# Where ScalarE's steps of a weight split stand in its queue, and how many blocks are split early

## The chip, the cores and the metric

One core of one Trainium2 chip. The metric is the device time of one execution in microseconds (us). TensorE does the matrix products, VectorE and ScalarE and GpSimd the elementwise work, SyncE (SP) issues nearly all DMAs. Each engine works through its own queue in program order and waits there for what its next instruction needs.

## What is computed

```python
def reference(q, k, v, moe_w_in, moe_w_out, moe2_...):
    # attention, 4 batches x 8 heads, 1152 keys, 576 queries (pairs of q rows averaged), head size 64
    q_pool = q.reshape(B, H, S // 2, 2, D).mean(axis=3)
    p = softmax(q_pool @ k.T / sqrt(D))
    x = (p @ v) as [2304 tokens, 512]
    # dense layers, 512 -> 2048 -> 512, weights are 64-bit floats
    h = x @ w_in
    x = (h * sigmoid(1.702 * h)) @ w_out
    # eight experts, 512 -> 1024 -> 512, for the tokens with x @ w_skip > 0
    y[token] = gate * (relu(x @ w1[e]) @ w2[e]) for e = argmax(x @ w_gate)
    return x + y
```

## The kernel before

Every matrix operand is kept as a high and a low float32 part, and a product is three matmuls (high x high, high x low, low x high). The weights of the dense layers come as 64-bit floats and must first be **split** into such pairs. DFF = 2048 is cut into 16 blocks fb; a block needs one piece of w_in (giving the tiles wih, wil) and one of w_out (woh, wol). These 32 pieces are the units u = 2 fb + k, 128 x 512 numbers each. `wload` brings a unit into one of three buffers wr by DMA on SP's queue, `wsplit` splits it: ten instructions, seven on VectorE (L463, L464, L451, L466, L467, L455, L459 in this order) and three on ScalarE: L461 (the absolute value into t2, first), L452 (the low part's scale, on what L451 has just made) and L458 (the high part's rounding, on what L467 made). `wsplit` issues L461 at once and returns seven functions; L452 is issued together with L451 by `low`, L458 together with the last VectorE instruction by `last`.

**Attention** runs over 16 pairs of heads, 14 units of work each. One loop over steps g of 14 x 16 and some more writes out the order by hand: in each step the score matmuls of a unit (L273, into one of two banks), the exponential (L274, ScalarE), the maxima of a later pair (L230, L233), the products with v of an earlier unit (L310), sums of E for the denominators (L288, L290, L69, GpSimd; on VectorE for the end of the last pair), and the denominators' matmuls (L326). `Agenda` holds further work to be issued at a given step: among it the early units of the split. With EARLY = 3 blocks, units 0 and 1 are spread over quiet steps of pairs 1 to 9, and units 2 to 5 over the last 19 steps and the two behind, five steps each. Each instruction stands in its engine's queue where the loop issues it.

**The dense layers** go over six chunks of tokens (768, 384, 256, 256, 256, 384). A step g is one piece of up to 384 tokens and one block fb; the first chunk has two pieces, so 32 steps. In a step `layer1` issues 12 matmuls (L577) into one of two banks h, then on ScalarE the sigmoid (L582), on VectorE g (L583), on ScalarE gh (L584), on VectorE gl (L586); `layer2` issues 9 matmuls (L601 to L603) for the piece of two steps before. In the first chunk the other units are split on the way: `fill(3)` ahead of gl and `fill(3)` or `fill(4)` behind it take the next functions of `blocks()`, which goes through the units in order and holds back the last two functions of a unit (L455; L458 and L459) into the next one. That is 13 functions per block fb, and 26 units have 182. From step 23 on the x tiles of the next chunk are loaded (SP), normalised by VectorE (L482) and split (L491, L495). Behind the first chunk the split's buffers are given up, and the gate weights (wg) are loaded into their place.

**The experts** come last and are not touched.

Of the kernel before, what the change touches and what calls it, by code (L numbers as in the profile page):

```python
# [9 lines left out]
F32 = mybir.dt.float32  # L10
# [9 lines left out]
P = 128  # L20
# [29 lines left out]
EARLY = 3  # L50
# [21 lines left out]
class Kernel:  # L72
# [54 lines left out]
    def attention(self, ctx):  # L127
# [217 lines left out]
        def weights(u, put):  # L345
            t = ld.tile([P, 3, 512], U32, name="t", tag="wt", bufs=1)
            for j, f in enumerate(self.wsplit(u, [t[:, 0], t[:, 1], t[:, 2]])):
                put(j, f)
# [8 lines left out]
        for u in range(2):  # L357
            g = NU * 1 + 3 + u * (NU * 3 + 6)
            ag.at(g, self.wload, u)
            ag.at(g + 6, weights, u, lambda j, f: quiet(AV_AT[3:], j, f))  # L360

        for u in range(2, 2 * EARLY):
            g, n = NU * (N - 1) - 5, u - 2
            ag.at(g - 13 + 4 * n if n < 3 else g + 7, self.wload, u)
            ag.at(g + 5 * n, weights, u, lambda j, f, g=g + 5 * n: ag.at(g + j * 5 // 7, f))
# [64 lines left out]
    def wsplit(self, u, tmp):  # L430

        nc, V = self.nc, self.nc.vector
# [4 lines left out]
        if a.dtype == F32:  # L439
# [4 lines left out]
            ]  # L444
# [4 lines left out]

        def low():  # L450
            V.scalar_tensor_tensor(t1, lo, 9, t1, op0=ALU.logical_shift_right, op1=ALU.bitwise_or)  # L451
            nc.scalar.activation(t1.bitcast(F32), t1, AF.Copy, scale=2.0 ** -43)  # L452

        def power():
            V.tensor_scalar(sg, t2, 0xFF800000, None, op0=ALU.bitwise_and)  # L455

        def last():
            nc.scalar.activation(hi_t, t2.bitcast(F32), AF.Copy)  # L458
            V.tensor_tensor(lo_t, t1.bitcast(F32), sg.bitcast(F32), op=ALU.mult)  # L459

        nc.scalar.activation(t2.bitcast(F32), hi.bitcast(F32), AF.Abs)  # L461
# [3 lines left out]
            low,  # L465
            lambda: V.tensor_scalar(t2, t2, 3, 0x3FFFF000, op0=ALU.logical_shift_left, op1=ALU.bitwise_and),  # L466
            lambda: V.scalar_tensor_tensor(t2, hi, 0xC0000000, t2, op0=ALU.bitwise_and, op1=ALU.bitwise_or),  # L467
            power,
            last,
# [27 lines left out]
    def ffn(self, ctx):  # L497
# [36 lines left out]
        def blocks():  # L534

            end = ()
            for u in range(2 * EARLY, 2 * NF):
                if u + 2 < 2 * NF:
                    self.wload(u + 2)
                a, b, c, d, e, *new = self.wsplit(u, [tp.tile([P, 512], U32, name=nm, tag=nm) for nm in ("t1", "t2", "sg")])  # L540
                yield from (a, *end[:1], b, c, d, *end[1:], e)
                end = new
            yield from end

        splits = blocks()

        def fill(k):
            for _ in range(k):
                f = fq.pop(0) if fq else next(splits, None)
                if f:  # L550
                    f()

# [503 lines left out]
```

## Time and profile before

| | us |
|---|---|
| median of 3 runs | 1069.68 |
| lowest and highest | 1064.24, 1069.93 |
| the profiled execution | 1067.2 |
| its span, first to last instruction | 1065.1 |
| TensorE busy | 1002.7 (94% of the span) |
| VectorE busy | 767.6 (72%) |
| ScalarE busy | 506.0 (48%) |
| GpSimd busy | 453.5 (43%) |
| mean granted TensorE clock | 0.980 of 2.4 GHz |

The profile is of one execution. Rows name the line, the engine (PE is TensorE, DVE VectorE, ACT ScalarE, POOL GpSimd), the operation, and output <- inputs by the program's names. Matmuls are pipelined, so their durations overlap, and a step is better read from the starts. A row of the timeline ends with the idle time ahead of it on its engine, and who ended it.

### The profile page before, as it was taken

To read this page: it belongs to the slowest core of one execution; us is meant where nothing else is said; L and a number is where in the kernel's file an instruction comes from. 1 tells how busy PE (TensorE), PEld (TensorE's weight loads), DVE (VectorE), ACT (ScalarE), POOL (GpSimd) and SP (SyncE) were. 2 spreads that over 40 slices of the span, in tenths; PEclk is the share of its full clock that TensorE was granted. 3 is DMA by queue.
4 is the path that set the end of the run, shared out by engine and by line. 5 is a ranking of instruction groups with operands and counts; after the bars stand their busy time and mean duration, and the time that the engine had idled before them with its cause. 6 is when DMAs were issued, how large, how long until landed. Compare 5 with 4: busy or idle time off the path is not lost. (4 is left out here: it accounts for less than half of the span.)

```text
span 1065.1 us, 19053 instructions
## 1 busy us (share of the span) xinstructions
PE 1002.7 (94%) x7002; PEld 789.9 (74%) x7002; DVE 767.6 (72%) x1643; ACT 506.0 (48%) x928; POOL 453.5 (43%) x306
## 2 busy tenths in 40 slices
PE   6999999999999998799998999999999997998894
PEld 4666767666776665587887898888889886866673
DVE  7667777778877778878988589787475564556834
ACT  2555555555555554555655322333333262456623
POOL 3698999999999988400000002011111004213112
PEclk9999999999999999999999999999999998998997
DMA  4232232223333321323333620212211234738401
GB/s 161 69 100 80 80 100 80 80 80 95 95 96 98 101 87 62 101 80 115 120 99 99 169 79 22 70 30 59 70 47 45 80 116 152 249 123 272 150 22 50
DMA packets 64323, 103.38 MB, mean 97 GB/s; under 512 B 18630, under 2 KB 34630, under 8 KB 64072
## 3 DMA queue, kind: packets, MB, share of 16 engines
q1 hardware_dynamic: 60148, 96.35, 28.5%
q0 software_dynamic: 3904, 5.15, 1.6%
q8 instruction: 69, 1.13, 0.5%
q14 instruction: 54, 0.44, 0.1%
q10 hardware_dynamic: 148, 0.30, 0.1%
HBM read 90.04 MB, written 17.35 MB: 101 GB/s over the span
## 5 line engine op out<-in xcount | busy, mean ns | idle before, releaser
L233 DVE TENSOR_REDUCE mx<-xs 128x1 f32<-128x384 f32 x432 | 212.9, 550 | 81.1 <-PE xs L230 76.7
L274 ACT ACTIVATE E<-ss 128x640 f32<-128x640 f32 (+1 forms) x224 | 174.1, 786 | 148.0 <-PE ss L273 125.3
L290 POOL TENSOR_TENSOR acc<-acc,E 128x640 f32<-128x640 f32 (+1 forms) x94 | 179.8, 1912 | 22.4 <-ACT E L274 18.6
L310 PE MATMUL av<-E,v 128*64 128x256 f32 (+1 forms) x1152 | 158.5, 415 | 0.0
L577 PE MATMUL h<-xh,wih 128*128 128x384 f32 (+1 forms) x448 | 142.7, 318 | 8.7 <-DVE g L583 6.3
L577 PE MATMUL h<-xl,wih 128*128 128x384 f32 (+1 forms) x448 | 140.7, 314 | 0.2
L577 PE MATMUL h<-xh,wil 128*128 128x384 f32 (+1 forms) x448 | 140.5, 314 | 0.0
L482 POOL TENSOR_TENSOR xa<-xraw 128x256 f32<-128x256 f32 (+1 forms) x16 | 14.2, 890 | 256.9 <-DMA xraw<-RD 251.4
L310 PEld LDWEIGHTS av<-E,v 128*64 128x64 f32 x1152 | 76.3, 137 | 56.8 <-issue 16.4
L603 PE MATMUL acc<-woh,gl 128*128 128x512 f32 x288 | 114.7, 398 | 0.0
L601 PE MATMUL acc<-woh,gh 128*128 128x512 f32 x288 | 114.5, 398 | 0.0
L602 PE MATMUL acc<-wol,gh 128*128 128x512 f32 x288 | 114.3, 397 | 0.0
L273 PE MATMUL ss<-qh,kh 64*128 64x320 f32 (+1 forms) x576 | 107.1, 339 | 7.7 <-ACT E L274 7.7
L230 PE MATMUL xs<-kh,qh 64*128 64x384 f32 x384 | 102.9, 390 | 7.8 <-ACT kh L210 7.2
L577 PEld LDWEIGHTS h<-xh,wih 128*128 128x128 f32 x448 | 84.9, 190 | 18.8 <-DVE g L583 11.1
L583 DVE TENSOR_TENSOR g<-h,g 128x384 f32<-128x384 f32 (+1 forms) x112 | 55.8, 498 | 59.4 <-ACT g L582 58.0
L273 PE MATMUL ss<-M,ONE 64*128 64x320 f32 (+1 forms) x576 | 95.1, 296 | 2.8 <-DMA M<-ml 2.6
L584 ACT ACTIVATE gh<-g 128x384 fp32r<-128x384 f32 (+1 forms) x112 | 53.8, 480 | 89.9 <-DVE g L583 89.9
L620 DVE CUSTOM_DVE_ANT_0 junk<-xs,wg 128x512 bf16<-128x512 f32 x135 | 94.8, 702 | 2.0
L582 ACT ACTIVATE g<-h 128x384 f32<-128x384 f32 (+1 forms) x112 | 49.2, 439 | 97.9 <-PE h L577 97.8
L273 PE MATMUL ss<-qh,kl 64*128 64x320 f32 (+1 forms) x576 | 92.6, 294 | 0.0
L273 PE MATMUL ss<-ql,kh 64*128 64x320 f32 (+1 forms) x576 | 92.6, 294 | 0.0
(195 smaller groups left out, 2070.2 us busy)
## 6 DMA issues: line engine op xcount, KB each, us to landing
stage<-w SPq DMA_DIRECT2D x40, 512.0 KB
qd<-qT SPq DMA_DIRECT2D x16, 576.0 KB
v<-v SPq DMA_DIRECT2D x16, 576.0 KB
kr<-kT SPq DMA_DIRECT2D x15, 576.0 KB
wr<-w_in SPq DMA_DIRECT2D x16, 512.0 KB
wr<-w_out SPq DMA_DIRECT2D x16, 512.0 KB
X<-xs SPq DMA_DIRECT2D x18, 256.0 KB
out<-xs SPq DMA_DIRECT2D x18, 256.0 KB
```

What stands on the lines that cost most here:

```text
L230: nc.tensor.matmul(ps[:, :384], q, k[:, part * 384:part * 384 + 384], start=True, stop=True)
L233: V.reduce_max(o, ps[:, :384], axis=AX.X)
L273: nc.tensor.matmul(ps[:, u, j * w:j * w + w], k[HALF[u]], q[HALF[u], qs], start=(n == 0), stop=(n == 3))
L274: nc.scalar.activation(place(p, i), ps[:, :, :len(kbs) * w], AF.Exp, scale=0.5 / D ** 0.5)
L290: G.tensor_tensor(d["a"], d["a"], place(p, i), op=ALU.add)
L310: nc.tensor.matmul(d["av"][HALF[u], :w], d["v"][:, u, kb], e[:, u, n * w:n * w + w], start=(kb == 0), stop=(kb == KB - 1))
L577: nc.tensor.matmul(h, a[:, d * P:d * P + P], x, start=(k == 0), stop=(k == 3 * ND - 1))
L583: V.tensor_tensor(g, h, g, op=ALU.mult)
L601: nc.tensor.matmul(acc[t], gh[:, ts], bh, start=(fb == 0), stop=False)
L602: nc.tensor.matmul(acc[t], gh[:, ts], bl, start=False, stop=False)
L603: nc.tensor.matmul(acc[t], gl[:, ts], bh, start=False, stop=(fb == NF - 1))
L620: V.tensor_tensor_reduce(out=junk, in0=R[grp[i]], in1=late["wg"][:, e], op0=ALU.mult, op1=ALU.add, scale=1.0, scalar=0.0, accum_out=R[grp] ...
```

## The change

EARLY becomes 2: units 2 and 3 are split in the last 20 steps of attention, eight steps apart, and the 28 units from fb = 2 on in the first chunk of the dense layers (196 functions of VectorE in place of 182). `wsplit` issues nothing itself; it returns VectorE's seven and ScalarE's three functions apart, and each caller places them. In attention, a unit's steps are: Abs at g - 1, VectorE's seven at g to g + 5 and g + 8, the low part's scale at g + 5 (three behind what makes its input), the high part's rounding at g + 7. The scratch tile gets two buffers. In the dense layers a list `after` collects ScalarE's functions when their inputs have been issued; `act()` issues all that are in it, in every step behind gh, and `need` does so earlier where VectorE's next function wants one that is still in the list. A unit is begun (`make`, with the load of the unit two ahead) in the middle of the one before it.

```diff
--- before.py
+++ after.py
@@ -47,7 +47,7 @@
 
 UNITS = [(0, (kb,)) for kb in range(KB)] + [(1, tuple(range(kb, min(kb + 2, KB)))) for kb in range(0, KB, 2)]
 NU = len(UNITS)
-EARLY = 3
+EARLY = 2
 AV_AT = (4, 7, 10, 13, 1)
 GROUPS = [range(0, 3), range(3, 6), range(6, 9), range(9, 12), range(12, 14)]
 
@@ -342,10 +342,11 @@
         start = {1: [(k_low, 0)], 2: [(q_low, 0)], 4: [(loads, 2)], 5: [(q_add, 1)], 7: [(q_high, 1)], 8: [(k_high, 1, 0)], 9: [(k_high, 1, 1)],
                  10: [(k_high, 1, 2)], 11: [(v_load, 0)], 13: [(q_add, 2)]}
 
-        def weights(u, put):
-            t = ld.tile([P, 3, 512], U32, name="t", tag="wt", bufs=1)
-            for j, f in enumerate(self.wsplit(u, [t[:, 0], t[:, 1], t[:, 2]])):
-                put(j, f)
+        def weights(u, steps):
+            t = ld.tile([P, 3, 512], U32, name="t", tag="wt", bufs=2)
+            v, a = self.wsplit(u, [t[:, 0], t[:, 1], t[:, 2]])
+            for g, f in zip(steps, (a[0], v[0], v[1], v[2], v[3], v[4], v[5], a[1], a[2], v[6])):
+                ag.at(g, f)
 
         def operands(j, pc):
             raw = ld.tile([P, 2, 384], F32, name="xraw", tag="xraw", bufs=1)
@@ -356,13 +357,14 @@
 
         for u in range(2):
             g = NU * 1 + 3 + u * (NU * 3 + 6)
+            calm = [x for x in range(g + 7, g + 5 * NU) if x % NU in AV_AT[3:]]
             ag.at(g, self.wload, u)
-            ag.at(g + 6, weights, u, lambda j, f: quiet(AV_AT[3:], j, f))
+            ag.at(g + 6, weights, u, [g + 6, *calm[:6], calm[4] + 1, calm[5] + 1, calm[6]])
 
         for u in range(2, 2 * EARLY):
-            g, n = NU * (N - 1) - 5, u - 2
-            ag.at(g - 13 + 4 * n if n < 3 else g + 7, self.wload, u)
-            ag.at(g + 5 * n, weights, u, lambda j, f, g=g + 5 * n: ag.at(g + j * 5 // 7, f))
+            g = NU * (N - 1) - 5 + 8 * (u - 2)
+            ag.at(g - 13, self.wload, u)
+            ag.at(g - 1, weights, u, [g - 1, g, g + 1, g + 2, g + 3, g + 4, g + 5, g + 5, g + 7, g + 8])
         for n in range(2):
             ag.at(NU * N - 8 + 5 * n, self.wload, 2 * EARLY + n)
         for b in range(8):
@@ -431,6 +433,7 @@
 
 
 
+
         nc, V = self.nc, self.nc.vector
         fb, k = divmod(u, 2)
         a = self.raws.pop(u)
@@ -441,32 +444,23 @@
                 none, none, none, none, none,
                 lambda: nc.scalar.activation(hi_t, a, AF.Copy),
                 lambda: V.tensor_tensor(lo_t, a, hi_t, op=ALU.subtract),
-            ]
+            ], [none, none, none]
         w = a.bitcast(U32).rearrange("p (n two) -> p n two", two=2)
         lo, hi = w[:, :, 0], w[:, :, 1]
         t1, t2, sg = tmp
         least = float(np.uint32(0x38000000).view(np.float32))
-
-        def low():
-            V.scalar_tensor_tensor(t1, lo, 9, t1, op0=ALU.logical_shift_right, op1=ALU.bitwise_or)
-            nc.scalar.activation(t1.bitcast(F32), t1, AF.Copy, scale=2.0 ** -43)
-
-        def power():
-            V.tensor_scalar(sg, t2, 0xFF800000, None, op0=ALU.bitwise_and)
-
-        def last():
-            nc.scalar.activation(hi_t, t2.bitcast(F32), AF.Copy)
-            V.tensor_tensor(lo_t, t1.bitcast(F32), sg.bitcast(F32), op=ALU.mult)
-
-        nc.scalar.activation(t2.bitcast(F32), hi.bitcast(F32), AF.Abs)
         return [
             lambda: V.tensor_scalar(t1, hi, 23, None, op0=ALU.logical_shift_left),
             lambda: V.tensor_scalar(t2.bitcast(F32), t2.bitcast(F32), least, None, op0=ALU.max),
-            low,
+            lambda: V.scalar_tensor_tensor(t1, lo, 9, t1, op0=ALU.logical_shift_right, op1=ALU.bitwise_or),
             lambda: V.tensor_scalar(t2, t2, 3, 0x3FFFF000, op0=ALU.logical_shift_left, op1=ALU.bitwise_and),
             lambda: V.scalar_tensor_tensor(t2, hi, 0xC0000000, t2, op0=ALU.bitwise_and, op1=ALU.bitwise_or),
-            power,
-            last,
+            lambda: V.tensor_scalar(sg, t2, 0xFF800000, None, op0=ALU.bitwise_and),
+            lambda: V.tensor_tensor(lo_t, t1.bitcast(F32), sg.bitcast(F32), op=ALU.mult),
+        ], [
+            lambda: nc.scalar.activation(t2.bitcast(F32), hi.bitcast(F32), AF.Abs),
+            lambda: nc.scalar.activation(t1.bitcast(F32), t1, AF.Copy, scale=2.0 ** -43),
+            lambda: nc.scalar.activation(hi_t, t2.bitcast(F32), AF.Copy),
         ]
 
     def xload(self, t, c, j, pc):
@@ -533,15 +527,40 @@
 
         def blocks():
 
-            end = ()
-            for u in range(2 * EARLY, 2 * NF):
+
+            def make(u):
                 if u + 2 < 2 * NF:
                     self.wload(u + 2)
-                a, b, c, d, e, *new = self.wsplit(u, [tp.tile([P, 512], U32, name=nm, tag=nm) for nm in ("t1", "t2", "sg")])
-                yield from (a, *end[:1], b, c, d, *end[1:], e)
-                end = new
-            yield from end
-
+                t = [tp.tile([P, 512], U32, name=nm, tag=nm, bufs=n) for nm, n in (("t1", 2), ("t2", 3), ("sg", 1))]
+                v, a = self.wsplit(u, t)
+                after.append(a[0])
+                return v, a
+
+            def need(f):
+                if f in after:
+                    act()
+
+            end, conv, new = (), None, make(2 * EARLY)
+            for u in range(2 * EARLY, 2 * NF):
+                v, a = new
+                yield v[0]
+                yield from end[:1]
+                need(a[0])
+                yield v[1]
+                yield v[2]
+                after.append(a[1])
+                yield v[3]
+                new = make(u + 1) if u + 1 < 2 * NF else None
+                need(conv)
+                yield from end[1:]
+                yield v[4]
+                after.append(a[2])
+                end, conv = v[5:], a[1]
+            yield end[0]
+            need(conv)
+            yield end[1]
+
+        after = []
         splits = blocks()
 
         def fill(k):
@@ -549,6 +568,10 @@
                 f = fq.pop(0) if fq else next(splits, None)
                 if f:
                     f()
+
+        def act():
+            while after:
+                after.pop(0)()
 
         xraw, xa = {}, {}
 
@@ -582,6 +605,7 @@
             nc.scalar.activation(g, h, AF.Sigmoid, scale=1.702)
             V.tensor_tensor(g, h, g, op=ALU.mult)
             nc.scalar.activation(gh, g, AF.Copy)
+            act()
             fill(fa)
             V.tensor_tensor(gl, g, gh, op=ALU.subtract)
             fill(fb_)
@@ -753,7 +777,9 @@
                 layer2(c2, f2, p2)
                 if f2 == NF - 1:
                     if c2 == 0 and p2 == 0:
-                        fill(14)
+                        while splits.gi_frame:
+                            fill(1)
+                            act()
                         rctx.close()
                         late["o"] = self.pool(ctx, "m_o", 2)
                         late["wg"] = late["o"].tile([P, 9, DM], F32, name="wg", tag="wg", bufs=1)
```

## Rows read from the trace of the kernel before

**Rows 1.** Busy time in windows: PE, PEld, DVE, ACT, POOL, PEclk, DMA, GB/s.
```profile
410.00:456.00 46.00, 35.19 (x335) 22.88 (x332) 38.66 (x43) 25.73 (x41) 27.15 (x25) 0.96 0.21 67
420.00:425.00 5.00, 5.00 (x44) 3.22 (x42) 3.56 (x2) 1.16 (x3) 4.92 (x3) 0.83 0.00 0
455.00:460.00 5.00, 4.74 (x19) 4.31 (x20) 0.22 (x2) 0.83 (x2) 0.00 (x0) 0.66 0.16 60
...
575.00:580.00 5.00, 5.00 (x19) 4.49 (x18) 5.00 (x12) 3.65 (x7) 0.00 (x0) 0.66 0.21 71
```

**Rows 2.** Waits of the whole span: us in total, times, longest.
```profile
PE ss L273 <- ACT E L274: 7.7, 5, 2.8
```

**Rows 3.** Timeline, 413 to 418 us: start, us, engine, line, operation, tiles, [idle before].
```profile
413.45 2.38 POOL L288 TENSOR_TENSOR acc<-E 128x1024 f32<-128x1024 f32 x1
...
413.74 2.64 DVE L451 SCALAR_TENSOR_TENSOR t<-wr,t 128x512 uint32<-128x512 uint32 x1
...
416.42 0.63 ACT L452 ACTIVATE t<-t 128x512 f32<-128x512 uint32 x1 [2.74 <-DVE t L451]
...
418.01 0.39 PE L273 MATMUL ss<-qh,kh 64*128 64x256 f32 x2 [2.73 <-ACT E L274]
```

**Rows 4.** Timeline of VectorE and TensorE, end of attention.
```profile
451.53 0.42 DVE L455 TENSOR_SCALAR t<-t 128x512 uint32<-128x512 uint32 x1
451.98 0.69 DVE L459 TENSOR_TENSOR wol<-t 128x512 fp32r<-128x512 f32 x1
...
453.55 0.71 PE L326 MATMUL dn<-ds,one 128*64 128x288 f32 x4 [2.14 <-DVE ds L69]
455.26 0.71 PE L326 MATMUL dn<-ds,one 128*64 128x288 f32 x4 [1.00 <-DVE mac L529]
```

**Rows 5.** Timeline of TensorE: first matmul of steps 3, 32, 33 and 34.
```profile
465.88 0.34 PE L577 MATMUL h<-xh,wih 128*128 128x384 f32 x1
...
596.88 0.34 PE L577 MATMUL h<-xh,wih 128*128 128x384 f32 x1
...
603.36 0.34 PE L577 MATMUL h<-xh,wih 128*128 128x384 f32 x1
...
607.55 0.34 PE L577 MATMUL h<-xh,wih 128*128 128x384 f32 x1
```

**Rows 6.** Timeline of ScalarE, three sigmoids and one L452.
```profile
556.74 0.47 ACT L582 ACTIVATE g<-h 128x384 f32<-128x384 f32 x1
...
561.64 0.47 ACT L582 ACTIVATE g<-h 128x384 f32<-128x384 f32 x1
...
566.35 0.63 ACT L452 ACTIVATE t<-t 128x512 f32<-128x512 uint32 x1 [1.85 <-DVE t L451]
566.89 0.47 ACT L582 ACTIVATE g<-h 128x384 f32<-128x384 f32 x1
```

**Rows 7.** Timeline of VectorE back to back, and g in step 33.
```profile
514.09 0.55 DVE L583 TENSOR_TENSOR g<-h,g 128x384 f32<-128x384 f32 x1
514.56 0.68 DVE L451 SCALAR_TENSOR_TENSOR t<-wr,t 128x512 uint32<-128x512 uint32 x1
515.16 0.42 DVE L466 TENSOR_SCALAR t<-t 128x512 uint32<-128x512 uint32 x1
515.50 0.68 DVE L459 TENSOR_TENSOR wil<-t,sg 128x512 fp32r<-128x512 f32 x1
516.10 0.55 DVE L586 TENSOR_TENSOR gl<-g,gh 128x384 fp32r<-128x384 f32 x1
...
606.22 0.56 DVE L583 TENSOR_TENSOR g<-h,g 128x384 f32<-128x384 f32 x1 [2.23 <-ACT g L582]
```

**Rows 8.** Timeline of VectorE and TensorE at the next chunk's x tiles.
```profile
573.20 0.56 DVE L482 TENSOR_TENSOR xa<-xraw 128x384 f32<-128x384 f32 x1 [2.23 <-DMA xraw<-RD]
...
574.28 0.44 PE L577 MATMUL h<-xh,wih 128*128 128x384 f32 x1 [1.81 <-DVE g L583]
...
599.05 0.56 DVE L482 TENSOR_TENSOR xa<-xraw 128x384 f32<-128x384 f32 x1 [4.43 <-DMA xraw<-RD]
```

## The prediction

> **What bounds the kernel now.** I read the engine rows of the page first: TensorE is busy for 94% of the span, so only stretches where it idles, or where its clock is halved, can give time back. The busy time in equal windows finds two such stretches beside the start and the expert part: the end of attention (410 to 456 us) and the first chunk of the dense layers (466 to 607 us). In the first, TensorE is busy for 35.2 of 46 us, and ran part of that at 1.2 GHz [rows 1].
>
> Next the table of waits: TensorE's score matmuls (L273) waited 7.7 us in 5 pieces for ScalarE's exponentials [rows 2]; asked for 380 to 465 us alone the table has the same row, so all five lie there. One of them in order of time shows the chain: GpSimd's addition of 2.38 us starts, VectorE's L451 starts 0.29 us later and takes 2.64 us; ScalarE, whose queue is in order, sits 2.74 us in L452, with exponentials behind it whose scores are ready; TensorE then has both score banks full and idles 2.73 us [rows 3]. ScalarE is not short of time, it is stopped by the order of its queue. That is the wait that ends last here.
>
> In the dense layers the same pair makes a loop. One step g (12 matmuls of layer 1 for piece g, 9 of layer 2 for piece g-2) takes TensorE 4.19 us when nothing holds it (603.36 to 607.55) [rows 5]. From the start of step 3 (465.88) to that of step 32 (596.88) are 29 steps: 29 x 4.19 = 121.4 us, taken 131.0, so 9.6 us are lost; step 32 loses 6.48 - 4.19 = 2.3 more. The ScalarE rows show why: L452 waits 1.85 us for VectorE, and the sigmoid of the next piece runs only behind it; sigmoid to sigmoid is 4.90 and 5.25 us, against 4.19 for TensorE [rows 6]. VectorE alone is not the bound: back to back, its instructions follow each other after 0.47 (g), 0.60 (L451), 0.34 (L466) and 0.60 us (L459) [rows 7]. A unit's seven are four of 0.34 and three of 0.60, 3.16 us; 6.5 of 7 fall in a step, 2.9 us, with g and gl (0.47 each) 3.9, under 4.19.
>
> **The change part by part.**
>
> *Attention, ScalarE's steps spread out.* The activation of the low part now stands three agenda steps behind the VectorE step that it needs, the rounding of the high part also three, and Abs one step ahead of the first VectorE step. TensorE's 35.2 busy us are some 19 agenda steps [rows 1], 1.8 us each, so three are 5 us, against the 2.64 us of the slow L451 [rows 3]. I take the whole 7.7 us as gone [rows 2]. The lower bound: the waits stay and only two of the four late units go, half, 3.8.
> VectorE's L451 took 2.64 us beside GpSimd, and takes 0.68 in the dense layers, where GpSimd rests [rows 3, 7]. The Trainium skill (SBUF — State Buffer, Who interferes with whom) says that a VectorE instruction with two SBUF inputs and a GpSimd instruction that reads SBUF exclude each other for the whole of one; the rows agree. By that rule the slow L451 stays in the two units that are left, but is never longer than one GpSimd instruction allows, and the sum is the same.
>
> *Attention, one unit less at its very end.* Behind the last exponential VectorE adds up the denominators, with instructions of the sixth unit between: L455 and L459 hold its queue for 0.45 and, as elsewhere, 0.60 us, while TensorE idles 2.14 + 1.00 us [rows 4, 7]. They go, and no L452 holds up the last exponentials. Between 1.1 and 3.1 I take 2.3 us.
>
> *Clock.* 420 to 425 us ran at 0.83 of full speed and 455 to 460 at 0.66, both behind idle stretches: 0.17 x 5 + 0.34 x 5 = 2.6 us [rows 1]. With most of the idle time gone I take 2.4, between 0 and 2.6. Attention together: 7.7 + 2.3 + 2.4 = 12.4 us.
>
> *Dense layers, ScalarE's steps behind gh.* They now stand at one place of a step, behind gh, and use VectorE results of the step before, so the sigmoid waits for nothing of its own step. In some steps the next unit's Abs is wanted at once and forces the pending ones early; VectorE has by then passed what they need, by two of its instructions or more. The 9.6 us are open to gain, and I subtract what is late next:
>
> *Two more units in the first chunk.* 28 units are 196 VectorE instructions (182 before). Steps take 6 and 7 in turn, 13 per block of DFF, and each block of DFF needs 14: the supply falls one behind for each, and the last wih and wil come late. The last instruction of the b-th of them (from 0) is number 7b + 11. For fb = 15, b = 26, it is number 193, the fifth of step 29. VectorE starts g 2.86 us behind the start of TensorE's step (603.36, 606.22) [rows 5, 7]; then 0.47, two of 0.34, one of 0.60, gl 0.47, one of 0.34, and 0.68 until it is written: 6.1 us, 1.9 into step 30. wil is wanted two of a step's 21 matmuls in, at 0.4: a wait of 1.5 us. In the same way fb = 14 (number 179, fourth of step 27) waits 1.2, fb = 13 (165, third of step 25) 0.4, earlier ones not at all. Together 3.1 us that nothing hides. Bounds: 0 (VectorE ahead of this) and 6.5 (two of the waits followed by a halved clock, 1.7 us each as in 575 to 580 us [rows 1]).
>
> *The x transfers.* VectorE's product of the first x tile of the next chunk (L482) waited 2.23 us for its DMA, behind it g, and TensorE 1.81 us; 575 to 580 us ran at 0.66 [rows 8, 1]: 1.81 + 1.7 = 3.5 us. The load's place in SP's queue hardly moves: it stands behind a weight load, which now waits for the current unit's L467, issued one VectorE instruction later. With shorter steps there is less time from load to use. So I let 3.5 us stay, between 0 and 5. Net of the three: 9.6 - 3.1 - 3.5 = 3.0 us.
>
> *Step 32.* It waited for the fourth x tile, VectorE 4.43 us for its transfer [rows 8]. Behind that load SP issues the gate weights, spread to all partitions, as soon as the split buffers are free. These come free in step 30 now, not 28, so the tile travels alone: 2.3 us gained [rows 5], bound 0. No row shows what the later gate weights cost; three steps lie between them and their first use in step 33, and I take 0, at most 2 us.
>
> *At no cost:* the second buffer of the scratch tile (6 KB per partition, against 8 KB that the third pair of matrices gives back); the first two units, since TensorE waited for no exponential outside the end part [rows 2]; the loads in attention, two fewer on SP's queue.
>
> Sum: 12.4 + 3.0 + 2.3 = 17.7 us. The profiled execution took 1067.2 us (span 1065.1), 0.2% under the median 1069.7. 1067.2 - 17.7 = 1050 us.
>
> **The rivals.**
> *A. Attention's waits stay.* VectorE could fall more than three steps behind, since a contended instruction takes up to 2.6 us and a step 1.8. Against it: seven instructions now have eight steps, not five. Half of the 7.7, 1.1 at the end, nothing of the clock: 4.9 + 3.0 + 2.3 = 10.2, 1057 us.
> *B. Nothing is late in the dense layers.* If VectorE runs ahead and the x transfers fit: 12.4 + 9.6 + 2.3 = 24.3, 1043 us. Against it: the count of 193.
> *C. Slower: the loop stays and takes in the whole first chunk.* If the pending ScalarE steps, run early for Abs, wait for a VectorE instruction of the same step, every piece pays the round of ScalarE and VectorE, at worst 5.25 us [rows 6]: 29 x (5.25 - 4.19) = 30.7 in place of 9.6, and the late weights then wait for a lag of a whole step and more, about 6 us: 1067.2 - 12.4 + 21.1 + 6 = 1082. It decides from a mean step of 4.75 us on, where 29 x 0.56 + 6 eats 12.4 + 9.6. Against it: what the pending steps need is two or more VectorE instructions old.
> *D. No change.* ScalarE is busy for only 25.7 of the 46 us, VectorE for 38.7 [rows 1]; what ScalarE's order gives back, VectorE would take at the next wait: 1067 us. Against it: TensorE's 7.7 us name ScalarE, and VectorE has gaps too. The Trainium skill (Perfetto Trace Analysis, Identifying the Most-Contended Engine) says to work first on the engine with the highest occupancy, which would leave ScalarE alone and speaks for this rival; the trace speaks against it, since TensorE stood still for an engine that was idle itself [rows 3].
>
> **How the numbers follow.** Forecast 0.58 (1050; its own bounds 1045 to 1056), A 0.14 (1057), B 0.14 (1043), C 0.06 (1082), D 0.08 (1067). The range for 8 in 10 goes from below B, 1041, to beyond A, 1061; C and D are left out. 0.5%, about what a measurement of this kernel can tell, is 5.3 us from 1069.7: forecast, A and B are faster (0.86), D the same (0.08), C slower (0.06).
>
> **What the profile will show.** Right: no wait of TensorE for E above 0.5 us at the end of attention; ScalarE's wait for VectorE ahead of the low part gone from both stretches; sigmoids 4.19 us apart through most of the first chunk; waits of layer 1 at steps 26, 28 and 30 of 0.4, 1.2 and 1.5 us. Wrong: sigmoids 4.75 us apart and more (C), idle TensorE of 2 us and more between 410 and 440 us (A), or no wait at steps 26 to 30 (B).

## The result, and the profile after

| | before | after |
|---|---|---|
| median, us | 1069.44 (4 runs, 1064.24 to 1069.93) | 1080.55 (4 runs, 1079.25 to 1087.42) |
| the profiled execution, its span | 1067.2, 1065.1 | 1079.25, 1077.5 |
| attention: start of the dense layers, step 0 | 455.9 | 446.4 |
| steps 3 to 32, 29 x 4.19 = 121.4 when nothing holds them | 131.0 (9.6 lost) | 157.4 (36.0 lost) |
| step 32, 4.19 when nothing holds it | 6.48 | 4.19 |

The ratio is 1.0111, with a 95% interval of 1.0084 to 1.0138: the change makes the kernel slower by 1.1%, where 1.8% faster was forecast. Attention and step 32 gave about what was forecast (9.5 us and 1.5 more up to step 3, where 12.4 were forecast; 2.3 for 2.3); the first chunk of the dense layers lost 26.4 us more than before.

Line numbers are now those of the kernel after: VectorE's seven instructions of a split are L453 to L459, in this order; ScalarE's three are L461 (Abs), L462 (the low part's scale) and L463 (the high part's rounding, which writes wih or woh). In a step, layer 1 is L600, the sigmoid L605, g L606, gh L607, gl L610; the product of an x tile is L476. In runs with other edits the lines behind the splits shift by a few. The page's engine row of after has TensorE no less busy, in a longer span:

```profile
PE 1007.1 (93%) x7002; PEld 793.1 (74%) x7002; DVE 768.1 (71%) x1643; ACT 502.5 (47%) x928; POOL 452.8 (42%) x306
```

Timeline of TensorE, after: first matmuls of steps 3, 32 and 33, the lines that answer to [rows 5].

```profile
454.83 0.34 PE L600 MATMUL h<-xh,wih 128*128 128x384 f32 x1
...
612.24 0.34 PE L600 MATMUL h<-xh,wih 128*128 128x384 f32 x1
...
616.43 0.34 PE L600 MATMUL h<-xh,wih 128*128 128x384 f32 x1
```

End of attention, after: the wait for E (380 to 447 us; total, times, longest), for [rows 2], and the denominators' matmuls, for [rows 4].

```profile
PE ss L273 <- ACT E L274: 2.1, 4, 1.5
```
```profile
444.76 0.66 PE L326 MATMUL dn<-ds,one 128*64 128x288 f32 x4
445.74 0.71 PE L326 MATMUL dn<-ds,one 128*64 128x288 f32 x4 [0.33 <-DVE mac L523]
```

The wait for E fell from 7.7 to 2.1 us, the two idle times ahead of the denominators from 3.1 to 0.3. Now the first chunk, after: waits from 454 to 616 us.

```profile
DVE t L454 <- ACT t L461: 20.1, 17, 1.7
...
PE h L600 <- ACT wih L463: 12.1, 6, 4.1
...
PE h L600 <- DVE wil L459: 9.6, 5, 4.3
DVE xa L476 <- DMA xraw<-RD: 6.1, 2, 4.2
```

Two kinds of wait have grown. VectorE stands 20.1 us, in 17 pieces, ahead of L454, the maximum that takes what Abs (L461) has made; TensorE stands 21.7 us ahead of layer 1 for weights that are not yet split. Before, in the same window, TensorE did not wait for weights, and VectorE's wait for Abs (L464 was the maximum) was this:

```profile
DVE t L464 <- ACT t L461: 2.7, 5, 0.8
```

The first kind in order of time, after, VectorE and then ScalarE in the same 9 us:

```profile
507.17 0.55 DVE L606 TENSOR_TENSOR g<-h,g 128x384 f32<-128x384 f32 x1
509.38 0.43 DVE L454 TENSOR_SCALAR t<-t 128x512 f32<-128x512 f32 x1 [1.66 <-ACT t L461]
...
510.66 0.55 DVE L610 TENSOR_TENSOR gl<-g,gh 128x384 fp32r<-128x384 f32 x1
...
513.00 0.55 DVE L606 TENSOR_TENSOR g<-h,g 128x384 f32<-128x384 f32 x1
515.22 0.43 DVE L454 TENSOR_SCALAR t<-t 128x512 f32<-128x512 f32 x1 [1.67 <-ACT t L461]
```
```profile
507.75 0.53 ACT L607 ACTIVATE gh<-g 128x384 fp32r<-128x384 f32 x1 [2.42 <-DVE g L606]
508.18 0.62 ACT L462 ACTIVATE t<-t 128x512 f32<-128x512 uint32 x1
508.71 0.64 ACT L461 ACTIVATE t<-wr 128x512 f32<-128x512 f32 x1
509.25 0.62 ACT L463 ACTIVATE woh<-t 128x512 fp32r<-128x512 f32 x1
509.78 0.47 ACT L605 ACTIVATE g<-h 128x384 f32<-128x384 f32 x1
513.59 0.53 ACT L607 ACTIVATE gh<-g 128x384 fp32r<-128x384 f32 x1 [3.34 <-DVE g L606]
```

VectorE makes g at 507.17. ScalarE's gh waits for that g, behind gh stand the pending scale (L462) and Abs, and VectorE's next instruction wants this very Abs: it stands still from 507.72 to 509.38. So this step holds a round of g, gh, L462, Abs and L454, and g to g takes 5.83 us. ScalarE in turn sits 3.34 us ahead of the next gh. VectorE's own work would fit into 4.19 us (4.09 in i1, below), but not with a wait beside it; each engine waits for the other. Of before, [rows 6, 7] show the opposite: ScalarE waited in L452, and VectorE ran back to back.

### The profile page after: what moved, and what is told of

Same layout as the page of the kernel before. It is cut to its first block, busy times and chain, and to the rows that moved or that the text cites. A ratio compares the mean times of both kernels' runs of the same rounds, so it can differ in the third digit from the quotient of the medians.

```text
span 1077.5 us, 19071 instructions
## 1 busy us (share of the span) xinstructions
PE 1007.1 (93%) x7002; PEld 793.1 (74%) x7002; DVE 768.1 (71%) x1643; ACT 502.5 (47%) x928; POOL 452.8 (42%) x306
## 5 line engine op out<-in xcount | busy, mean ns | idle before, releaser
L290 POOL TENSOR_TENSOR acc<-acc,E 128x640 f32<-128x640 f32 (+1 forms) x94 | 179.5, 1909 | 16.4 <-ACT E L274 12.4
L600 PE MATMUL h<-xh,wih 128*128 128x384 f32 (+1 forms) x448 | 143.9, 321 | 14.6 <-ACT wih L463 12.1
L600 PE MATMUL h<-xh,wil 128*128 128x384 f32 (+1 forms) x448 | 143.0, 319 | 9.6 <-DVE wil L459 9.6
L600 PE MATMUL h<-xl,wih 128*128 128x384 f32 (+1 forms) x448 | 142.0, 317 | 0.1
L476 POOL TENSOR_TENSOR xa<-xraw 128x256 f32<-128x256 f32 (+1 forms) x16 | 14.4, 902 | 284.7 <-DMA xraw<-RD 284.7
L230 PE MATMUL xs<-kh,qh 64*128 64x384 f32 x384 | 102.9, 390 | 7.9 <-ACT kh L210 7.3
L607 ACT ACTIVATE gh<-g 128x384 fp32r<-128x384 f32 (+1 forms) x112 | 53.7, 480 | 119.4 <-DVE g L606 119.4
L605 ACT ACTIVATE g<-h 128x384 f32<-128x384 f32 (+1 forms) x112 | 49.4, 441 | 122.7 <-PE h L600 122.6
L600 PEld LDWEIGHTS h<-xh,wih 128*128 128x128 f32 x448 | 85.9, 192 | 24.5 <-ACT wih L463 15.7
L606 DVE TENSOR_TENSOR g<-h,g 128x384 f32<-128x384 f32 (+1 forms) x112 | 55.6, 497 | 60.0 <-ACT g L605 58.4
L600 PEld LDWEIGHTS h<-xh,wil 128*128 128x128 f32 x448 | 86.1, 192 | 11.2 <-DVE wil L459 11.2
```

Of the source, the lines that this page charges most:

```text
L230: nc.tensor.matmul(ps[:, :384], q, k[:, part * 384:part * 384 + 384], start=True, stop=True)
L290: G.tensor_tensor(d["a"], d["a"], place(p, i), op=ALU.add)
L600: nc.tensor.matmul(h, a[:, d * P:d * P + P], x, start=(k == 0), stop=(k == 3 * ND - 1))
L606: V.tensor_tensor(g, h, g, op=ALU.mult)
```

## The experiments

Each is the changed kernel with the edit shown; ratios are to runs of the kernel before on the same chip. "Lost" is steps 3 to 32 less 121.4 us, in the profiled execution. All in one table first:

| order of ScalarE's steps in the dense layers | VectorE functions per two steps | lost, us | ratio, 95% interval |
|---|---|---|---|
| of the change (the kernel after) | 13 | 36.0 | 1.0111, 1.0084 to 1.0138 |
| of the change, third block early (e1) | 13 | 15.8 | 1.0104, 1.0052 to 1.0157 |
| of before (e2) | 13 | 22.0 | 0.9965, 0.9936 to 0.9995 |
| of before, and in attention too (g2) | 13 | 22.9 | 0.9946, 0.9921 to 0.9972 |
| Abs a step ahead, load moved with it (e3) | 13 | 33.9 | 1.0069, 1.0046 to 1.0092 |
| the same, third block early (e4) | 13 | 9.8 | 0.9999, 0.9972 to 1.0025 |
| Abs a step ahead, loads in place (f3) | 13 | 18.4 | 0.9922, 0.9891 to 0.9953 |
| of the change (f2) | 14 | 48.8 | 1.0251, 1.0228 to 1.0274 |
| Abs a step ahead (f4) | 14 | 4.0 | 0.9824, 0.9798 to 0.985 |
| Abs a step ahead, x earlier (h1) | 14 | 0.1 | 0.9798, 0.9748 to 0.9848 |
| of before (h2) | 14 | 6.1 | 0.9843, 0.9798 to 0.9889 |
| of before, x earlier (i2) | 14 | 0.0 | 0.9826, 0.9781 to 0.987 |
| of the change, shifted by two (i1) | 14 | 1.5 | 0.9848, 0.9806 to 0.9889 |

**Theory** after the result: VectorE's wait for an Abs behind gh makes the round. **Rival:** two units more, 14 functions wanted for 13 given, make the weights late, whatever the order.

**e1_three_early.** The third block back into attention, its four last units ten steps apart and earlier (room for one scratch tile only).

```diff
-EARLY = 2
+EARLY = 3
-            t = ld.tile([P, 3, 512], U32, name="t", tag="wt", bufs=2)
+            t = ld.tile([P, 3, 512], U32, name="t", tag="wt", bufs=1)
-            g = NU * (N - 1) - 5 + 8 * (u - 2)
+            g = NU * (N - 1) - 27 + 10 * (u - 2)
```

> The changed kernel, but with three early blocks again (units 2 to 5 ten agenda steps apart from step 183 of attention on, one scratch buffer), so that the first chunk splits 26 units. Theory A (the Abs stands behind gh and the pending ScalarE steps, so VectorE's L454 waits for it, and the step becomes a round of VectorE and ScalarE): VectorE's waits for the Abs stay near 20 us and steps of 5.1 to 5.5 us stay, but the weights are no longer late: 1060 to 1066 us. Theory B (28 units are more than the first chunk supplies in time, whatever ScalarE's order): TensorE's waits for wih and wil (21.7 us) vanish and the steps are near 4.19 us: about 1052 us.

Lost 15.8 us: no wait for weights is left, Abs still costs VectorE 18.0 us, as theory A wants. But both times were missed (1083 us): attention ended at 457.0, not 446.4, and step 32 took 10.40 us. Waits of TensorE from 24 to 446 us and busy time (PE, PEld, DVE, ACT, POOL) from 380 to 400 us:

```profile
PE xs L230 <- DVE mx L233: 7.1, 10, 1.8
```
```profile
380.00:400.00 20.00, 16.45 (x146) 10.51 (x145) 19.90 (x27) 8.42 (x12) 16.52 (x9) 0.96 0.11 30
```

VectorE has no gap there for two units more: the maxima come late, and TensorE waits for those in place of E (0.6 us left).

**e2_old_dense_order.** The dense layers' order of before, with 28 units; the place where a unit begins, its load and the scratch buffers go back with it.

```diff
-                after.append(a[0])
+                a[0]()
+                def low(v=v, a=a):
+                    v[2]()
+                    a[1]()
+                def last(v=v, a=a):
+                    a[2]()
+                    v[6]()
...
-                yield v[2]
-                after.append(a[1])
+                yield low
...
-                after.append(a[2])
-                end, conv = v[5:], a[1]
+                end = [v[5], last]
```

> The changed kernel with its attention and two early blocks, but with ScalarE's three steps in the dense layers placed as before (Abs at the head of the unit, low part right behind L455, high part just ahead of L459). Theory A: the waits of VectorE for the Abs are as few as before (2 us), the first chunk loses what it lost before (9.6 us) and some 5 us for late weights: about 1062 us. Theory B: 28 units are late in this order too, 20 us of waits for wih and wil: 1073 us and more.

Waits from 440 to 625 us, TensorE and ScalarE:

```profile
PE h L593 <- ACT wih L463: 14.5, 7, 4.3
```
```profile
ACT t L462 <- DVE t L455: 28.8, 24, 1.9
```

22.0 us are lost with the old order too, and its wait for weights is 14.5 us: the rival is part of it. The change's order costs 14 us more (36.0). Neither side's figure held: theory A had 14.6 us lost, theory B 20 us of waits for weights.

**g2_early_two_alone.** As e2, and in attention the low part's scale and the rounding back to their old places as well; Abs stays a step ahead there.

```diff
-            ag.at(g + 6, weights, u, [g + 6, *calm[:6], calm[4] + 1, calm[5] + 1, calm[6]])
+            ag.at(g + 6, weights, u, [g + 6, *calm[:6], calm[2], calm[6], calm[6]])
...
-            ag.at(g - 1, weights, u, [g - 1, g, g + 1, g + 2, g + 3, g + 4, g + 5, g + 5, g + 7, g + 8])
+            ag.at(g - 1, weights, u, [g - 1, g, g + 1, g + 2, g + 3, g + 4, g + 5, g + 2, g + 8, g + 8])
...
```

> Two early blocks alone: ScalarE's three steps placed as before, in attention (low part right behind L455, high part just ahead of L459) and in the dense layers; only the eight steps per unit are kept. Attention's end tells whether the room or the order gave the 9.5 us: the first layer 1 starts at 446 to 448 us if the two units less did it, at 452 us or later if the order of ScalarE's steps did it. The first chunk loses as much as e2_old_dense_order (22.0 us).

Waits of TensorE and ScalarE from 380 to 447 us:

```profile
PE ss L273 <- ACT E L274: 2.2, 5, 1.4
```
```profile
ACT t L462 <- DVE t L455: 4.5, 2, 3.3
```

Attention ends at 447.1 us, as with the change's order (446.4 to 449.3 in the ten kernels that have it with two blocks early). ScalarE does sit 3.3 us in L462 again, yet TensorE's waits for E stay at 2.2 us. So attention's gain did not come from the places of L462 and L463. Abs a step ahead, which g2 keeps, does not give it alone either: e1 has it, with the rest of the change's order and ten steps for a unit (but one scratch buffer), still splits four units there, and ends attention at 457.0 us, where the kernel before did at 455.9. What is left is the two units less; room for a unit was not varied by itself.

**e3_abs_ahead.** The next unit begins, with its Abs and its load, at the front of a unit and not in its middle.

```diff
                 yield v[0]
+                new = make(u + 1) if u + 1 < 2 * NF else None
...
                 yield v[3]
-                new = make(u + 1) if u + 1 < 2 * NF else None
```

> The changed kernel with one edit in the dense layers: the next unit is begun (its load and its Abs) behind the first VectorE step of a unit, not behind the fourth, so that the Abs is issued a step before VectorE wants it. Theory A: VectorE's waits for the Abs fall from 20.1 us to under 3, most steps take 4.19 us, and only the late weights of the last blocks (some 3 us) and the x tile stay: 1052 to 1056 us. Theory B: the count of units and of slots is the same, so wih and wil stay late by some 20 us: 1070 us and more.

Waits for Abs fell to 5.4 us, yet 33.9 us were lost: `make` also issues a weight load, which now stands in SP's queue waiting for its buffer, ahead of the x loads. VectorE waited 16.3 us for x tiles (longest 8.6), and TensorE 23.7 us for wih behind it. **f3_abs_ahead_same_loads** leaves the loads where the change has them:

```diff
-                if u + 2 < 2 * NF:
-                    self.wload(u + 2)
...
+            self.wload(2 * EARLY + 2)
...
                 yield v[0]
+                new = make(u + 1) if u + 1 < 2 * NF else None
...
                 yield v[3]
-                new = make(u + 1) if u + 1 < 2 * NF else None
+                if u + 3 < 2 * NF:
+                    self.wload(u + 3)
```

> The Abs a step earlier as in e3_abs_ahead, but the weight loads left at their place in SP's queue (in e3_abs_ahead the load moved too, and x loads stood behind it). Theory A: the loss of the first chunk falls from 36.0 to some 8 us. Theory B: TensorE's waits for wih go on from step 16 or so, loss 18 to 25 us. If the load was what held e3_abs_ahead up, the wait of VectorE for the x tiles (16.3 us there) is back at 6 us.

Waits from 440 to 625 us, TensorE and VectorE:

```profile
PE h L601 <- ACT wih L463: 11.9, 6, 4.4
```
```profile
DVE t L454 <- ACT t L461: 5.4, 7, 1.0
```

VectorE's wait for x tiles fell from 16.3 to 4.6 us, so the load was what held e3 up. Half of the loss goes with Abs; what stays, 18.4 us as theory B wants, is mostly the wait for weights.

**e4_abs_ahead_three_early.** The edits of e1 and e3 together:

```diff
-EARLY = 2
+EARLY = 3
...
                 yield v[0]
+                new = make(u + 1) if u + 1 < 2 * NF else None
```

> The edits of e1_three_early and e3_abs_ahead together. Theory A: only the 3 us of late weights less than e3_abs_ahead: about 1050 us. Theory B: as e1_three_early, 1052 us, and 15 us and more below e3_abs_ahead.

9.8 us lost, 8.5 of them in the two steps that waited for x tiles (10.62 and 6.26 us long; VectorE's waits for x 12.8 us); attention, ending at 460.9, gave back what the chunk gained, and step 32 took 6.21 us. Both forecast times were missed (1074 us). Attention's code is that of e1, which ended it at 457.0: its end varies by some us from run to run.

**f2_seven_per_step.** The rival alone: 14 functions in two steps, as many as the units want.

```diff
-                    fa, fb_ = 3, 3 + pc
+                    fa, fb_ = 3, 4
```

> The changed kernel with one edit: every step of the first chunk takes seven VectorE instructions of the splits (3 ahead of gl, 4 behind), not six and seven in turn; 14 per block of DFF, as many as it needs. Theory B (supply): the last units no longer fall behind, TensorE's waits for wih and wil (21.7 us) go to under 4 us, and the first chunk loses 12 us or less instead of 36.0: about 1056 us. Theory A (the Abs stands behind gh and the pending ScalarE steps): seven instructions and the Abs wait of 1.3 us make a step of 5.4 us: the chunk loses 30 us or more: 1075 us and more.

No wait for weights is left, and it is the slowest of all, as theory A wants: L454 waits 28 times (from 440 to 625 us), and nearly every step up to 25 takes 5.83 us. The waits, and VectorE from one g to the next:

```profile
DVE t L454 <- ACT t L461: 45.7, 28, 1.7
```
```profile
507.92 0.55 DVE L606 TENSOR_TENSOR g<-h,g 128x384 f32<-128x384 f32 x1
510.13 0.43 DVE L454 TENSOR_SCALAR t<-t 128x512 f32<-128x512 f32 x1 [1.66 <-ACT t L461]
...
513.75 0.56 DVE L606 TENSOR_TENSOR g<-h,g 128x384 f32<-128x384 f32 x1
```

**f4_abs_ahead_seven.** f3's and f2's edits together:

```diff
                 yield v[0]
+                new = make(u + 1) if u + 1 < 2 * NF else None
...
-                    fa, fb_ = 3, 3 + pc
+                    fa, fb_ = 3, 4
```

> The edits of f2_seven_per_step and f3_abs_ahead_same_loads together. Theory B with A as a second, smaller part: no waits for weights, no waits for the Abs, steps of 4.19 us but for the x tile: loss 6 to 10 us, 1050 us, faster than the kernel before by 1.5 to 2%.

Faster than both kernels. Steps take 4.19 us up to step 25; what is lost, 4.0 us and 5.8 more in step 32 (10.01 us), stands at the x tiles (waits of VectorE, 440 to 625 us):

```profile
DVE xa L476 <- DMA xraw<-RD: 10.5, 3, 4.7
...
DVE t L454 <- ACT t L461: 0.8, 1, 0.8
```

**h1_ahead_seven_x_earlier** adds to f4:

```diff
-                            ag.at(g0, xload, c + 1, j, q)
+                            ag.at(g0 - (c == 0), xload, c + 1, j, q)
```

> The changed kernel with Abs a step ahead, seven VectorE functions in every step, and the four loads of the next chunk's x tiles issued one step earlier. What was left of the first chunk's loss with the first two edits stood at the x tiles: VectorE waited 10.5 us in 3 pieces for their transfers, steps 3 to 32 lost 4.0 us and step 32 another 5.8. Theory, the transfer is only issued too late: with a step (4.2 us) more the waits fall under 3 us, steps 3 to 32 lose under 2, step 32 under 2, ratio 0.975 (0.971 to 0.979). Rival, the transfer is short of bandwidth beside the weight loads that now run in the same steps: the waits stay at 8 us and more, ratio 0.980 to 0.985.

Steps 3 to 32 lost 0.1 us, as the theory wants; but the waits for x came down to 5.9 us only, 4.2 of them for the fourth tile, and step 32 took 8.56 us, 4.4 lost where the theory gave it under 2. The ratio's interval overlaps the ranges of both sides. What holds the fourth tile shows in i2, below.

**h2_old_order_seven.** e2's and f2's edits:

```diff
-                after.append(a[0])
+                a[0]()
...
-                    fa, fb_ = 3, 3 + pc
+                    fa, fb_ = 3, 4
```

> The changed kernel with the order of before in the dense layers (Abs when a unit begins, the low part's scale right behind its input, the rounding beside the last VectorE instruction) and seven VectorE functions in every step, so that no unit can come late. It prices the order of ScalarE's steps by itself. Theory of two causes: with the supply right, only the order's own round is left, sigmoids up to 4.9 us apart in the steps where the low part's scale waits for its input; steps 3 to 32 lose 8 to 12 us (the 9.6 of the kernel before), no wait for wih or wil over 1 us, ratio 0.985 to 0.990; the change's order with Abs ahead would then be worth 4 to 8 us, and the change's order as it stands (48.8 us lost with seven per step) is worse than the old by some 38 us. Rival, the old order also pays a whole round in every step once VectorE has seven functions in each: 20 us lost and more, ratio over 0.995.

Both sides were wrong: not 8 to 12 us lost by the old order's round, but none outside the x tiles (6.1 in all). L462 still waits 28 times, but 12.1 us in all and 1.1 at most (28.8 in e2), and every step up to 25 takes 4.19 us. So the old order's round, of which the prediction had made the 9.6 us of before, is no property of the order alone. But f2, which begins its steps at the very same place of a unit, lost 48.8 us: at this place the order is worth 43 us. (The kernel before with seven functions a step was not run, so how much it would gain by that alone is not shown.) With seven functions a step, a unit's seven always begin at the same place of a step; with 13 in two steps the place moves back by one every two steps. In the kernel after, L454 is among the first three functions of a step, between g and gl, in steps 0 to 4, again in 13 to 18 and in 27 to 29 (the first unit has five functions, every other seven; steps take 6 and 7 in turn). VectorE's waits for Abs stand in exactly these steps, 0.8 to 1.7 us each, and, at 0.5 us, in the two steps behind each of the first two stretches. The long steps are 3 to 6 (5.1 to 6.2 us) and 15 to 20, one or two behind; 9 to 14 take 4.19 (from 26 on x tiles and weights are late as well). That gives a theory that can be tested: for the change's order, the place decides.

**i1_seven_shifted_by_two.** f2, the worst of all, with two functions taken ahead of step 0:

```diff
         constants()
+        fill(2)
...
-                    fa, fb_ = 3, 3 + pc
+                    fa, fb_ = 3, 4
```

> The changed kernel, its order untouched, with seven VectorE functions in every step as in f2_seven_per_step, and two functions more taken once ahead of step 0. A unit has seven, so every step now begins at the same place of a unit: in f2 at L454, which is the first thing behind g and needs an Abs that stands behind the gh of that g; here two functions later, at L456, so that L454 comes behind gl, six VectorE instructions (2.7 us) behind g. Theory, the place of a unit at which a step begins decides, not the order of ScalarE's steps as such: VectorE's 45.7 us of waiting for Abs fall under 2, the steps are 4.19 us but for the x tiles (some 4 to 6 us lost, and some 6 in step 32), ratio 0.980 to 0.987, against 1.025 in f2. Rival, Abs behind gh and the pending steps costs its round wherever a step begins: steps of 5 us and more, over 25 us lost, ratio over 1.0.

Timeline of VectorE, one whole step of i1:

```profile
509.40 0.55 DVE L606 TENSOR_TENSOR g<-h,g 128x384 f32<-128x384 f32 x1
509.87 0.42 DVE L456 TENSOR_SCALAR t<-t 128x512 uint32<-128x512 uint32 x1
510.20 0.69 DVE L459 TENSOR_TENSOR wol<-t,sg 128x512 fp32r<-128x512 f32 x1
510.81 0.68 DVE L457 SCALAR_TENSOR_TENSOR t<-wr,t 128x512 uint32<-128x512 uint32 x1
511.41 0.55 DVE L610 TENSOR_TENSOR gl<-g,gh 128x384 fp32r<-128x384 f32 x1
511.88 0.42 DVE L453 TENSOR_SCALAR t<-wr 128x512 uint32<-128x512 uint32 x1
512.22 0.42 DVE L458 TENSOR_SCALAR sg<-t 128x512 uint32<-128x512 uint32 x1
512.55 0.42 DVE L454 TENSOR_SCALAR t<-t 128x512 f32<-128x512 f32 x1
512.89 0.68 DVE L455 SCALAR_TENSOR_TENSOR t<-wr,t 128x512 uint32<-128x512 uint32 x1
513.49 0.55 DVE L606 TENSOR_TENSOR g<-h,g 128x384 f32<-128x384 f32 x1
```

L454 stands seventh behind g, 2.6 us behind the end of g; Abs is done by then, and VectorE goes from g to g in 4.09 us without a gap. Its waits for Abs came to 2.7 us in one piece, ahead of step 3 (under 2 was expected), against 45.7 in 28; 1.5 us were lost, and 3.5 in step 32. ScalarE's queue has the same order as in f2 (gh, L462, Abs, L463, sigmoid). Two functions taken earlier, once, are worth 4% by the ratios (1.0251, 0.9848; medians 1101.4 and 1052.8 us, on two chips). The same rows say why every wait counted: 4.09 us of a step's 4.19 are VectorE's own work at seven functions, so f2's 1.66 us of waiting make 5.8.

**i2_old_order_seven_x_earlier.** h1's edit on h2, so that it differs from h1 by the order, with the place where a unit begins, its load and the scratch buffers that go with it.

```diff
-                            ag.at(g0, xload, c + 1, j, q)
+                            ag.at(g0 - (c == 0), xload, c + 1, j, q)
```

> h2_old_order_seven with the loads of the next chunk's x tiles one step earlier, as in h1_ahead_seven_x_earlier: it differs from h1 by the order of ScalarE's steps in the dense layers alone. Theory, with the supply right and a fixed place at which each step begins the order is worth nothing: nothing lost in steps 3 to 32 but under 1 us, ratio 0.977 to 0.983, as h1's 0.9798. Rival, the order with Abs ahead is worth 4 us and more of its own: ratio 0.984 and more.

Nothing lost up to step 32, and a ratio whose interval overlaps h1's: no worth of Abs ahead can be told from none, though 0.984, where the rival begins, lies inside the interval too. Step 32 took 11.56 us. SP's queue and the busy time (PE, PEld, DVE, ACT, POOL, PEclk, DMA share, GB/s) around it in i2, then SP's queue in after:

```profile
573.42 0.50 SPq L83 DMA_DIRECT2D xraw<-RD  x1
574.14 0.34 SPq L83 DMA_DIRECT2D wg<-wgT  x1
```
```profile
575.00:580.00 5.00, 5.00 (x27) 4.34 (x25) 2.07 (x5) 1.76 (x4) 0.00 (x0) 1.00 1.00 244
580.00:585.00 5.00, 0.27 (x2) 0.20 (x1) 0.78 (x2) 0.77 (x2) 0.00 (x0) 0.79 0.81 242
```
```profile
598.36 0.50 SPq L83 DMA_DIRECT2D xraw<-RD  x1
...
609.28 0.34 SPq L83 DMA_DIRECT2D wg<-wgT  x1
```

In i2 (and h1, i1, f4) the buffers are free early, so the gate weights follow the fourth x tile by 0.7 us; in i2 the DMA share is 1.00 from 575 to 580 us, TensorE stands still for most of 580 to 585 us, and its granted clock there is 0.79 of 2.4 GHz. In after they follow by 10.9 us, and step 32 loses nothing. All kernels here agree: in the nine where they follow within 0.8 us, before among them, step 32 takes 5.4 to 11.6 us; in the five where they follow by 7.2 us or more it takes 4.19. A kernel that has seven functions a step and holds the gate weights back was not tried; in h1 there are 8.56 - 4.19 = 4.4 us in step 32.

## Why the prediction was wrong, point by point

**Attention, 12.4 us: the size was right, the reason not.** 9.5 us up to step 0 and 1.5 up to step 3, 11.0. The step "I take the whole 7.7 us as gone" put them down to ScalarE's order. But g2 has L462 and L463 at their old places and nearly the same gain (447.1), and e1 has the new order, with E's waits gone (0.6 us left), and no gain. The rows had shown ScalarE sitting in L452 [rows 3], but the cure was to take work from VectorE where it is fullest; its "lower bound" (only two of the four late units go) named what mattered. VectorE was the busiest engine there, 38.7 of 46 us [rows 1]. The Trainium skill (Perfetto Trace Analysis, Identifying the Most-Contended Engine) says to work first on the engine with the highest occupancy. The prediction set that aside; g2 and e1 agree with it better than with the prediction. In the dense chunk busy time does not find the loss: it lies in a round between two engines. The last unit's removal was right (idle 3.1 to 0.3 us), and so was the clock: TensorE's granted clock was 1.00 from 400 to 460 us, in windows of 20, where before had 0.91 to 0.96.

**Step 32, 2.3 us: right**, in size and mechanism: the x tile travelled alone.

**Dense layers, +3.0 us forecast, -26.4 measured.** Two terms failed.

*"The 9.6 us are open to gain ... they use VectorE results of the step before, so the sigmoid waits for nothing of its own step."* That looked at ScalarE waiting for VectorE alone. The edge the other way was not priced: VectorE's L454 waits for an Abs that is now queued behind gh, and gh waits for VectorE's g of the same step. It waited 20.1 us in 17 pieces. Abs placed a step ahead gave back 17.6 us of loss (f3 against after); with seven functions a step, VectorE's functions placed elsewhere gave back 47.3 (i1 against f2). The sum "3.9, under 4.19" was read as room; it meant that VectorE had 0.3 us to spare in a step on the mean, and 0.1 at seven functions (4.09). In f2 a wait of 1.66 us made a step 1.64 us longer.

*"Together 3.1 us" for late weights.* Measured 21.7 us in 11 pieces. The count took only VectorE's last instruction, for wil, and a VectorE that is on time. But wih is written by ScalarE's L463, which the change issues behind the gh of a later step; 12.1 us were waits for it. The longest of these, at step 20, in VectorE, ScalarE and TensorE of after:

```profile
533.75 0.68 DVE L457 SCALAR_TENSOR_TENSOR t<-wr,t 128x512 uint32<-128x512 uint32 x1
...
540.01 0.52 ACT L607 ACTIVATE gh<-g 128x384 fp32r<-128x384 f32 x1 [2.59 <-DVE g L606]
540.44 0.61 ACT L463 ACTIVATE wih<-t 128x512 fp32r<-128x512 f32 x1
541.11 0.69 PE L600 MATMUL h<-xh,wih 128*128 128x384 f32 x1 [4.08 <-ACT wih L463]
```

L457 makes the rounding's input at 533.75, but L463 stands behind the gh of step 19, which needs step 19's layer 1; step 20 needs L463's wih. So this round passes through TensorE too. "Earlier ones not at all" failed as well: TensorE waited for wih at step 6 already (1.78 us), and for weights at steps 16, 18 and 20. Two units less (e1, e4) or seven functions a step (every run with 14) removed the whole term. The two terms go together: of the 36.0 us lost, f3 gave back 17.6, e1 20.2, and f4, which cures both, 32.0.

Behind the waits the clock was not granted in full either; windows of after, PEclk third from the end, of 2.4 GHz, so that part of each ran at 1.2 GHz:

```profile
570.00:575.00 5.00, 1.89 (x6) 1.89 (x7) 4.50 (x10) 2.34 (x4) 0.00 (x0) 0.68 0.04 14
575.00:580.00 5.00, 5.00 (x18) 4.34 (x17) 2.83 (x7) 1.01 (x2) 0.00 (x0) 0.64 0.50 163
```

TensorE had idled for 4.31 us ahead of 573.11. This is the price that the bound of 6.5 us had for two waits [rows 1]; it was charged more often: from 465 to 610 us, nine windows of 5 us of after are below 1.00, and one of before.

*x tiles, 3.5 us.* The waits stayed (6.1 us in 2 pieces, before 7.7 in 3), as forecast, but their longest, 4.2 us, also made wil late behind it in VectorE's queue: TensorE's longest wait for wil, 4.3 us, ended at 573.11, 2.6 us behind that tile's product.

**The rivals.** C had the time (1082 against 1080.55) and the place, a round of ScalarE and VectorE with late weights behind; its step of 5.25 was 5.43 on the mean, past the sign of 4.75 that the prediction had set. Its mechanism was turned round: not pending steps that wait for VectorE, but VectorE waiting for them. "What the pending steps need is two or more VectorE instructions old" was true but for two waits of 0.8 us and answered the wrong question, and with it went the chance of 0.06. That C's time came out so near is partly luck: late weights, which it had at 6 us, were 21.7. D's thought, that VectorE would take back what ScalarE's order gives, is what e1 shows in attention (L230's 7.1 us for the maxima in place of E's 7.7).

## What to carry to other kernels

When an instruction is moved in one in-order queue, list both kinds of edge: what it waits for, and who waits for what now stands behind something else; then follow each round trip between two engines and compare it with the step, not each engine's busy time with the step. Where a stream of small work is filled into a loop, give each step exactly as many pieces as it needs and choose at which piece a step begins: that made 1.025 or 0.985 out of the same order of ScalarE's steps. Place and order count together: at the place where this order was at its worst (f2), the old order and Abs a step ahead lost almost nothing outside the x tiles, and no difference between those two could be told. At the end of attention, taking work out of the stretch where VectorE has no gap gained; the new order of ScalarE's steps alone did not.

## What was not expected of the hardware

An x tile (two transfers of 192 KB) took 7.2 us from the issue of its second transfer to the product that waited for it (after: 563.3 to 570.50), more than a step of 4.19 us, and 9.7 us beside the gate weights (i2: 573.9 to 583.63). Issued one step ahead it was not hidden (VectorE waited 4.2 us for it); issued two steps ahead it left waits of 0.8 and 0.9 us (h1, 1.7 in sum), but for the tile that shares the DMA engines with the gate weights.
